# One load moved to another queue, a third of one product moved ahead of two transposes, and copied norm columns, in a fused attention and MLP kernel

## The chip, the cores and the metric

The kernel runs on one core of a Trainium2 chip. Its time is the device time of one execution in microseconds (us); the span is the part of it that the profile covers, about 1.4 us less. PE is TensorE, DVE is VectorE, ACT is ScalarE, POOL is GpSimd, SP is SyncE, which here only issues DMAs. All times inside a run are counted from the start of the span.

## The reference, cut to what matters

```python
xn = layernorm(x)                                  # x: 2048 tokens x 448
q, k, v = split(xn @ wqkv)                         # 16 heads of 28
pq, pk = phi(q), phi(k)                            # phi(t) = where(t > 0, t + 1, exp(t)) + 1e-6
s = (pq @ (pk.T @ v)) / (pq @ sum(pk)) @ wo        # per head, linear attention
g = silu(relu(xn @ w1 + b1) ** 2 @ w2 + b2)        # 448 -> 1792 -> 448
out = x + s * g
```

The change touches only the first 12 us: 16 tiles of 128 tokens are loaded, normalised and transposed, and the first products (K = xn times the k part of wqkv, H = xn times w1) start on the first tiles.

## The kernel before

The program is a list of operations; a small scheduler written in the kernel fixes the order on each engine, and semaphores carry the dependences. DVE and PE run their lists in order, so an operation that waits holds up all behind it. The loads at the start:

```python
load_x(0, 1)                                     # tile 0, 112 KB, on SP
load_x(1, 2, "act").prio = -118                  # tile 1 on ACT's queue
twins = load_k("sp", w_qkv, A_wqkv, "wk", 384, 2 * D, later=True)   # wk: rows 0 to 383
load_x(2, 4)
dma("act", b1r[...], B_b1 ...)
load_w1("w1a", 0, 512, 2, [twins])               # two halves, then last 64 rows of wk, of w1a
load_x(4, 8)
load_w1("w1b", 512, 1024)
```

448 columns are three chunks of 128 and one of 64. The last 64 columns are kept twice (columns 384 to 447 and 448 to 511), so that two half-height matmuls can run side by side (the traces show such pairs issued 3 to 4 ns apart). This "twin" is made in one instruction from x:

```python
def ln_last(si):                                 # writes both copies: 64 columns of x, read twice
    add("dve", tensor_scalar(out=xn[:, si, 384:512], in0=x_tok[...64 columns, twice], subtract mean, times rstd))
def ln_twin(lo, hi, eng="dve"):                  # tiles 4 to 15: a copy of the 64 normalised columns
    add(eng, tensor_copy(xn[:, lo:hi, 448:512], xn[:, lo:hi, 384:448]))
```

The head of PE's list, and the order that DVE is held to ("st" statistics, "mv" their mean and variance, "xn" norm, "xd" twin, "xT3" the eviction of tile 3's transposes):

```python
warm(8, wide=True)                               # dummy matmuls
turn(0, 0, "act"); turn(0, 1, "act")             # tile 0: 2 + 2 transposes, ACT evicts them
turn(1, 0, "act")                                # T10: first two chunks of tile 1
mains(k0, (0,), ...); mains(k0, (1,), ...); mains(k0, (2,), ...)    # K of tile 0, three chunks
turn(1, 1, "act")
mains(k1, (0, 1), ...) ...
h_mains(2); head["xT2"] = pe_transpose(2, None, "act")
h_mains(3); head["xT3"] = pe_transpose(3, None, "dve")
rests(k0, k1) ...                                # the last 64 rows of K and H
pe_four(*second)                                 # H for tiles 2 and 3; needs xT2, xT3
("dve", "st0 mv0 st1 mv1 xn00 xn01 xd0 xn10 xn11 xd1 st2 mv2 st3 mv3 xd2 xn2 xd3 xn3 xT3")
```

After xT3 the scheduler's DVE order is: st4, the min of phi(K0), st5, the min of phi(K1), the max-add of phi(K0), that of phi(K1). The max-add (a SCALAR_TENSOR_TENSOR) is the last reader of K0's PSUM bank (the memory, `pb` in the profiles, that holds the results of a phase's products until they are read). PE wants that bank for the phase of H4 and H6, just after that of K2 and K3 (Kn is K of tile n, Hn the n-th 128 of H's 1792 columns, both counted from 0).

## Time and profile before

| | before |
|---|---|
| three runs | 141.20, 141.24, 141.33 us |
| PE busy | 136.6 us of 139.7 (98%) |
| chain that ended last | PE 95% |
| tile 0 / wk / tiles 2-3 / tiles 4-7 landed | 2.20 / 4.07 / 4.73 / 8.76 us |

The landings are the last of a load's semaphore increments in the trace. Next come two lines of the page: the busy part, and the chain of waits followed back from the last instruction, as shares by engine.

```profile
PE 136.6 (98%) x1255; PEld 68.0 (49%) x1255; DVE 92.2 (66%) x226; ACT 77.8 (56%) x152; POOL 25.0 (18%) x33
...
PE 95%; DVE 2%; DMA 2%; issue 0%; DVEq 0%
```

PE is the limit, so what counts is the time at which PE stands idle or starts late. The timeline of PE at the start (start, length, engine, line, operation, operands, count, idle before it):

```profile
3.27 0.63 PE L1062 MATMUL pb<-ones 128*128 128x512 bf16 x1
4.09 1.00 PE L528 MATMUL pb<-ident,xn 128*128 128x128 bf16 x6 [0.19 <-DVE xn L486]
4.92 0.81 PE L641 MATMUL pb<-w_qkv,xT 128*128 128x512 bf16 x3
5.57 0.28 PE L528 MATMUL pb<-ident,xn 128*128 128x128 bf16 x2
5.68 0.59 PE L641 MATMUL pb<-w_qkv,xT 128*128 128x512 bf16 x2
```

The last dummy matmul, six transposes (four of tile 0 and T10), K of tile 0, two more transposes, K of tile 1. Lengths include the pipeline: a group of three 512-column matmuls "lasts" 0.81 us, but the next group starts 0.65 us after it.

DVE a little later, and PE beside it:

```profile
8.36 0.42 DVE L537 COPY xT<-pb 128x512 bf16<-128x512 bf16 x1 [0.49 <-PE pb L528]
8.78 0.63 DVE L463 BATCH_NORM_STATS2 st<-x_tok 128x6 f32<-128x448 bf16 x1
...
10.25 1.28 DVE L629 SCALAR_TENSOR_TENSOR qk<-pb,qk 128x512 bf16<-128x512 f32 x2
```

```profile
8.48 2.06 PE L688 MATMUL pb<-xT,w 64*128 64x256 bf16 x32
10.38 1.03 PE L641 MATMUL pb<-w_qkv,xT 64*128 64x512 bf16 x8
11.24 1.03 PE L688 MATMUL pb<-xT,w 64*128 64x512 bf16 x8
```

The statistics of tile 4 start at 8.78, when DVE has done the eviction before them; their load landed just before (8.76). The first max-add, from 10.25, frees K0's bank at 10.95.

### The profile page before, as it was taken

To read this page: it belongs to the slowest core of one execution; us is meant where nothing else is said; L and a number is where in the kernel's file an instruction comes from. 1 tells how busy PE (TensorE), PEld (TensorE's weight loads), DVE (VectorE), ACT (ScalarE), POOL (GpSimd) and SP (SyncE) were. 2 spreads that over 40 slices of the span, in tenths; PEclk is the share of its full clock that TensorE was granted. 3 is DMA by queue.
4 is the path that set the end of the run, shared out by engine and by line. 5 is a ranking of instruction groups with operands and counts; after the bars stand their busy time and mean duration, and the time that the engine had idled before them with its cause. 6 is when DMAs were issued, how large, how long until landed. Compare 5 with 4: busy or idle time off the path is not lost.

```text
span 139.7 us, 3106 instructions
## 1 busy us (share of the span) xinstructions
PE 136.6 (98%) x1255; PEld 68.0 (49%) x1255; DVE 92.2 (66%) x226; ACT 77.8 (56%) x152; POOL 25.0 (18%) x33
## 2 busy tenths in 40 slices
PE   9999999999999999999999999999999999999992
PEld 2474444444444444444455455645555555555481
DVE  3989899799878994889995900329636071542653
ACT  4769787879988878979788912422033030301220
POOL 6000000000000000000893000000002328091770
DMA  6997367999723200000000148960000103111122
GB/s 190 247 335 219 77 170 186 356 276 144 131 52 70 60 6 0 0 19 5 0 0 0 42 120 169 175 107 0 0 0 5 66 0 101 35 66 66 38 99 68
DMA packets 20354, 12.91 MB, mean 92 GB/s; under 512 B 9524, under 2 KB 19956, under 8 KB 20340
## 3 DMA queue, kind: packets, MB, share of 16 engines
q1 hardware_dynamic: 18332, 11.52, 33.3%
q10 hardware_dynamic: 2008, 1.20, 4.3%
q8 instruction: 10, 0.16, 0.5%
q14 instruction: 4, 0.03, 0.1%
HBM read 8.78 MB, written 2.10 MB: 78 GB/s over the span
## 4 chain that ended last, share of the span: by engine, by line
PE 95%; DVE 2%; DMA 2%; issue 0%; DVEq 0%
PE pb L955 31%; PE pb L688 30%; PE pb L641 9%; PE pb L1021 8%; PE pb L722 7%; PE pb L672 6%; DMA x_tok<-in_A_x_dram 2%; PE pb L528 1%; PE pb L728 1%; DVE st L463 1%; PE pb L815 1%; PE pb L776 1%; PE pb L853 0%; DVE xn L991 0%; DVE mv L464 0%; PE pb L846 0%
## 5 line engine op out<-in xcount | busy, mean ns | idle before, releaser
L688 PE MATMUL pb<-xT,w 64*128 64x512 bf16 (+2 forms) x408 | 51.6, 365 | 0.0
L955 PE MATMUL pb<-w,r 64*128 64x448 bf16 (+3 forms) x406 | 44.9, 343 | 0.0
L697 ACT ACTIVATE r<-pb,b1f 128x512 bf16<-128x512 f32 x56 | 35.1, 688 | 4.2 <-PE pb L688 4.2
L688 PEld LDWEIGHTS pb<-xT,w 64*128 64x128 bf16 (+1 forms) x408 | 22.8, 94 | 22.5 <-ACT r L697 0.5
L955 PEld LDWEIGHTS pb<-w,r 64*128 64x128 bf16 (+1 forms) x406 | 22.8, 95 | 19.9 <-issue 0.7
L966 DVE TENSOR_TENSOR gbuf<-pb,b2b 128x448 bf16<-128x448 f32 (+1 forms) x16 | 9.2, 608 | 30.0 <-PE pb L955 30.0
L931 ACT ACTIVATE gbuf<-gbuf 128x448 bf16<-128x448 bf16 (+1 forms) x16 | 8.7, 565 | 36.0 <-DVE gbuf L966 35.5
L1000 POOL TENSOR_TENSOR xn<-xn,x_tok 128x448 bf16<-128x448 bf16 x15 | 15.0, 1032 | 46.3 <-DVE xn L991 46.3
L641 PE MATMUL pb<-w_qkv,xT 64*128 64x512 bf16 (+1 forms) x106 | 17.8, 376 | 0.0
L672 PE MATMUL pb<-xT,w_qkv 64*128 64x512 bf16 x84 | 15.5, 376 | 0.0
L705 DVE TENSOR_TENSOR r<-r 128x512 bf16<-128x512 bf16 x42 | 14.4, 418 | 0.0
L390 POOL MEMSET kvm<- 128x2048 bf16 x1 | 1.8, 1804 | 63.4 <-DVE zb L666 63.4
L1021 PE MATMUL pb<-msb,pqT 64*128 64x448 bf16 (+3 forms) x93 | 10.9, 343 | 0.0
L629 DVE SCALAR_TENSOR_TENSOR qk<-pb,qk 128x512 bf16<-128x512 f32 x16 | 10.6, 685 | 0.2
L463 DVE BATCH_NORM_STATS2 st<-x_tok 128x6 f32<-128x448 bf16 x16 | 9.3, 610 | 2.0 <-DMA x_tok<-in_A_x_dram 2.0
L991 DVE TENSOR_TENSOR xn<-pb,gbuf 128x448 bf16<-128x448 f32 (+2 forms) x17 | 9.2, 591 | 2.0 <-ACT gbuf L931 1.5
L619 ACT ACTIVATE qk<-pb 128x512 bf16<-128x512 f32 x16 | 8.9, 593 | 3.0 <-PE pb L641 2.5
L641 PEld LDWEIGHTS pb<-w_qkv,xT 64*128 64x128 bf16 (+1 forms) x106 | 6.7, 94 | 6.0 <-ACT xT L538 0.2
L722 PE MATMUL pb<-qk,xn 128*128 128x448 bf16 x48 | 9.3, 353 | 0.0
L619 ACT ACTIVATE pqT<-pb 128x512 bf16<-128x512 f32 x12 | 6.8, 597 | 3.2 <-PE pb L688 1.6
L672 PEld LDWEIGHTS pb<-xT,w_qkv 64*128 64x128 bf16 x84 | 6.0, 94 | 5.0
L706 ACT ACTIVATE r<-r 128x512 bf16<-128x512 bf16 x14 | 8.4, 637 | 0.0
(71 smaller groups left out, 99.7 us busy)
## 6 DMA issues: line engine op xcount, KB each, us to landing
out_dram<-xn SPq DMA_DIRECT2D x15, 112.0 KB, 1.7
w<-in_B_w_dram SPq DMA_DIRECT2D x1, 1568.0 KB, 10.0
x_tok<-in_A_x_dram SPq DMA_DIRECT2D x3, 448.0 KB, 3.8
xT<-rows ACTq DMA_DIRECT2D x6, 112.0 KB
w<-in_B_w_dram SPq DMA_DIRECT2D x1, 576.0 KB, 4.6
xT<-rows SPq DMA_DIRECT2D x5, 112.0 KB
w_o<-in_A_wo_dram SPq DMA_DIRECT2D x1, 392.0 KB, 11.3
w_qkv<-in_A_wqkv_dram SPq DMA_DIRECT2D x1, 384.0 KB, 3.6
```

Source lines behind the costliest of these rows:

```text
L463: add("dve", lambda e, _: e.bn_stats(st6[:, si, :], x_tok[:, si, :]), [("x", si)], [("st", si)], 0.58),
L619: add("act", lambda e, _: e.activation(out=slot, in_=src(), func=AF.Exp), [buf, "actw"], [tile], 0.6)
L629: lambda e, _: e.scalar_tensor_tensor(out=slot, in0=src(), scalar=1.0 + 1e-6, in1=slot, op0=ALU.add, op1=ALU.max),
L641: return e.matmul(ps(b)[:, 0:512], xT[half[h], c, si * P : (si + 1) * P], w_qkv[half[h], c, 384 : 2 * D], start=start, stop=stop,)
L672: return e.matmul(ps(b)[:, 0:512], w_qkv[half[h], c, m * P : (m + 1) * P], xT[half[h], c, g * 512 : (g + 1) * 512], start=start, stop=stop,)
L688: return e.matmul(ps(b)[:, c0 : c0 + n], w_1[half[h], c, fi * P : (fi + 1) * P], xT[half[h], c, t : t + n], start=start, stop=stop,)
L697: lambda e, _: e.activation(out=slot, in_=ps(b)[:, 0:512], func=AF.Relu, bias=b1f[:, fi : fi + 1]),
L705: return e.tensor_tensor(out=slot, in0=slot, in1=slot, op=ALU.mult)
L722: last = e.matmul(ps(b)[:, 0:D], xn[:, si, c * P : (c + 1) * P], pk_of(si), start=(si == 0), stop=(si == NT - 1),)
L955: return e.matmul(ps(b)[:, 0:n], r2[half[h], fi, si * P : (si + 1) * P], w_2[half[h], fi, c], start=start, stop=stop)
L1000: eng, lambda e, _: e.tensor_tensor(out=ob, in0=ob, in1=x_tok[:, si, c], op=ALU.add),
L1021: return e.matmul(ps(b)[:, 0:n], q, m, start=start, stop=stop)
```

## The change

The intent: tile 0 should not share the DMA engines with tile 1 and land sooner; since tile 1 then comes later, a third of K0 fills the time ahead of its transposes; and copies of normalised columns should be cheaper than a second norm.

```diff
-        load_x(1, 2, "act").prio = -118
+        load_x(1, 2)
...
-            c = (slice(0, D if si > 3 else 384), slice(0, 256), slice(256, 384))[...]
+            c = (slice(0, D), slice(0, 256), slice(256, D if si else 384))[...]
...
-            twin = head[f"xd{i}"] = ln_last(i)
+            twin = head[f"xd{i}"] = ln_twin(i, i + 1, "dve") if i else ln_last(i)
...
         warm(8, wide=True)
+        warm(2)
...
+        mains(k0, (0,), [("xT", 0, "a")] + wnames("wk")[:1])
         turn(1, 0, "act")
-        mains(k0, (0,), [("xT", 0, "a")] + wnames("wk")[:1])
...
-            ("dve", "... st3 mv3 xd2 xn2 xd3 xn3 xT3"),
+            ("dve", "... st3 mv3 xn2 xd2 xn3 xd3 xT3"),
```

More of the change, by code (lines that the diff above doesn't have):

```diff
@@ L482, in ln_norm @@
         def ln_norm(si, part=None):
-            c = (slice(0, D if si > 3 else 384), slice(0, 256), slice(256, 384))[0 if part is None else part + 1]
+            c = (slice(0, D), slice(0, 256), slice(256, D if si else 384))[0 if part is None else part + 1]
             return add(
@@ L1108, in bass_recurrent_scan__linear_attn_block__dense_activation_squared_relu__prompt_kernel @@
         for eng, names in (
-            ("dve", "st0 mv0 st1 mv1 xn00 xn01 xd0 xn10 xn11 xd1 st2 mv2 st3 mv3 xd2 xn2 xd3 xn3 xT3"),
+            ("dve", "st0 mv0 st1 mv1 xn00 xn01 xd0 xn10 xn11 xd1 st2 mv2 st3 mv3 xn2 xd2 xn3 xd3 xT3"),
             ("act", "ln0 ex0 ln1 ex1 xT00a xT00 xT01 xT10 xT11 ln2 ex2 ln3 ex3 b1 xT2"),
```

## The prediction

> **What bounds it.** TensorE. The page gives PE 98% busy, the chain of waits 95% PE. From 8.8 us to the end I find no PE gap over 0.1 us in the matmul records, so only the first 8.8 us can move; a shift there should pass to the end one for one. That head (timeline, chain of waits) is: x tile 0 lands at 2.20; its statistics, Ln, Exp and normalise run to 4.04 (DVE/ACT); six transposes 4.09 to 4.92, each waiting for DVE; then PE is back to back (216 ns per 512-column matmul) from T10 at 4.80 to 8.16. Two fixed gaps follow: 0.10 us at 8.16, and 0.14 at 8.70, where PE waits for tile 3's eviction on DVE (8.36 to 8.78).
>
> **The queue move.** x tile 1 was issued on ACT at 0.16 us, its packets start at 1.53, while tile 0's run from 1.01 to 1.89. The Trainium skill (Trainium Kernel Development and Optimization, Key Constraints) says queues of different engines share the same 16 DMA engines and interleave; this trace agrees: both queues' packets are mixed from 1.53 to 1.85. Behind tile 0 on SP they cannot mix: estimate, three packets of 41 ns per engine, so tile 0 lands 0.12 us earlier (2.08), and tile 1 at 2.4 to 2.7, no later than the start of its statistics (2.98 before, about 2.86 then). Cost: one more issue of about 0.45 us on SP delays all later SP issues. wk 4.07 to about 4.4, x tiles 2-3 4.73 to 5.1, first w1 part 5.40 to 5.8, x tiles 4-7 8.76 to about 9.2. The first three should still be in time. Statistics of tile 4 already wait for their load (DVE at 8.78), so DVE there slips by 0.4; the K0 phi (ends 10.95) then releases its PSUM bank at 11.35, where PE wants it at 11.43. That slack is nearly eaten: 0 to 0.1 us.
>
> **The PE order.** K0's first third needs the xT eviction that ended at 4.79, so moving ahead of T10 gains only 0.07 us (4.92 to 4.85), while T10 moves from 4.80 to 5.07 and its eviction from 5.14-5.52 to 5.39-5.77. K1 then starts at 5.83 in place of 5.68: PE loses 0.14 us, to be set against tile 0's 0.12. Two narrow warm matmuls fill idle time, worth nothing.
>
> **The norm columns.** Tiles 1-3 replace a 0.31 us tensor_scalar by a 64-column copy (estimate 0.15 from the 0.20 of the 128-column copy), but it waits for the norm before it. For tiles 2, 3 the norm now comes first, so transposes may start 0.2 us earlier; yet PE reached those transposes late (slack 0.22 and 0.24), so it gains nothing.
>
> **Sum.** -0.12 + 0.14 + 0.03 = about +0.05; as DMA start-up may gain more than I count, I put it at 141.2 us, 140.9 to 141.55. Faster by over 2%: 0.01; within 2%: 0.98; slower: 0.01.
>
> **What would show it.** Tile 0 landing near 2.1; first transpose near 3.97; T10 after K0's first matmul; a 0.1 us gap before K1's first matmul; xn of tile 2 ahead of its twin and no PE wait there; statistics of tile 4 waiting to 9.2; a possible PE wait near 11.4.
>
> **What would make it wrong.** Tile 1 landing after 2.9, which delays tile 0's norm too, since DVE runs tile 1's statistics first. The TensorE clock: in the records matmuls run at half rate (427 ns per 512 columns) until about 4.8 us; K0's first third may fall in that stretch (+0.1 to 0.2). wk or x 2-3 landing later than 4.8 and 5.2.

## More of the kernel before

The waits of PE's weight loads (PEld) between 8 and 13 us are only this:

```profile
PEld pb L688 <- DVE xT L537: 0.3, 1, 0.3
```

## The result, and the profile after

Six runs of the changed kernel: median 141.66 us (141.41 to 141.71). Six of the kernel before: median 141.30 (141.20 to 141.58). The ratio is 1.0018, with a 95% interval of 1.0005 to 1.0031. A ratio here is the mean time of one kernel's fast runs over the mean of the other's in the same rounds, so it is not quite the ratio of the medians. The class "within 2%" was right; the time lay outside the stated range.

The same two lines of the page, of the changed kernel:

```profile
PE 136.9 (98%) x1257; PEld 68.5 (49%) x1257; DVE 92.1 (66%) x226; ACT 78.1 (56%) x152; POOL 25.0 (18%) x33
...
PE 97%; ACT 1%; DVE 0%; issue 0%; DVEq 0%
```

PE's timeline at the start:

```profile
3.27 0.85 PE L1062 MATMUL pb<-ones 128*128 128x512 bf16 x3
4.03 0.68 PE L528 MATMUL pb<-ident,xn 128*128 128x128 bf16 x4
4.74 0.39 PE L641 MATMUL pb<-w_qkv,xT 128*128 128x512 bf16 x1
4.96 0.28 PE L528 MATMUL pb<-ident,xn 128*128 128x128 bf16 x2
5.08 0.59 PE L641 MATMUL pb<-w_qkv,xT 128*128 128x512 bf16 x2
5.51 0.28 PE L528 MATMUL pb<-ident,xn 128*128 128x128 bf16 x2
5.72 0.60 PE L641 MATMUL pb<-w_qkv,xT 128*128 128x512 bf16 x2
```

Tile 0 landed at 2.15 instead of 2.20, so the transposes start 0.06 us sooner. K0's first third now stands before T10 (4.74). In the matmul records the last of the two transposes at 5.51 is issued at 5.564 and would be through in 0.053 us; K1 starts at 5.716, which is the 0.10 us gap foretold. K1 is 0.03 us later than before. DVE and PE further on:

```profile
8.39 0.42 DVE L537 COPY xT<-pb 128x512 bf16<-128x512 bf16 x1 [0.56 <-PE pb L528]
9.34 0.63 DVE L463 BATCH_NORM_STATS2 st<-x_tok 128x6 f32<-128x448 bf16 x1 [0.53 <-DMA x_tok<-in_A_x_dram]
...
10.80 1.28 DVE L629 SCALAR_TENSOR_TENSOR qk<-pb,qk 128x512 bf16<-128x512 f32 x2
```

```profile
8.51 2.06 PE L688 MATMUL pb<-xT,w 64*128 64x256 bf16 x32
10.41 1.03 PE L641 MATMUL pb<-w_qkv,xT 64*128 64x512 bf16 x8
11.54 1.04 PE L688 MATMUL pb<-xT,w 64*128 64x512 bf16 x8
```

Tiles 4-7 landed at 9.32. DVE stood idle 0.53 us for them, with phi(K0) behind it in line, and freed the bank at 11.50. PE's phase moved from 11.24 to 11.54. The waits of the weight loads, 8 to 13 us, have a new line:

```profile
PEld pb L688 <- DVE qk L629: 0.6, 1, 0.6
PEld pb L688 <- DVE xT L537: 0.3, 1, 0.3
```

0.6 us is the weight load's idle time. In the matmul records the lost time is 0.27 us: K2/K3's last matmul at 11.059 should be followed at 11.272, and is at 11.545. With the 0.03 of the head this is 0.30 of the 0.34 us by which the spans differ (139.65 and 139.99); from the bank phase to the last matmul the traces take 125.55 and 125.56 us. The page's chain of the changed kernel names an ACT instruction (L697) at this place instead of DVE; that instruction ended at 11.552, after the phase had started, so it cannot have released it. This pair of traces would close the case, but it was one pair, and it turned out to be an untypical one.

### The profile page after: what moved, and what is told of

It reads as the page before. It is cut to its first block, busy times and chain, and to the rows that moved or that the text cites. A ratio compares the mean times of both kernels' runs of the same rounds, so it can differ in the third digit from the quotient of the medians.

```text
span 140.0 us, 3110 instructions
## 1 busy us (share of the span) xinstructions
PE 136.9 (98%) x1257; PEld 68.5 (49%) x1257; DVE 92.1 (66%) x226; ACT 78.1 (56%) x152; POOL 25.0 (18%) x33
## 3 DMA queue, kind: packets, MB, share of 16 engines
HBM read 8.78 MB, written 2.10 MB: 78 GB/s over the span
## 4 chain that ended last, share of the span: by engine, by line
PE 97%; ACT 1%; DVE 0%; issue 0%; DVEq 0%
PE pb L955 30%; PE pb L688 30%; PE pb L641 8%; PE pb L1021 8%; PE pb L722 7%; PE pb L672 6%; PE pb L1062 3%; PE pb L728 1%; ACT r L697 1%; PE pb L528 1%; PE pb L815 1%; PE pb L776 1%; PE pb L853 0%; DVE xn L991 0%; PE pb L846 0%
## 5 line engine op out<-in xcount | busy, mean ns | idle before, releaser
L697 ACT ACTIVATE r<-pb,b1f 128x512 bf16<-128x512 f32 x56 | 35.2, 688 | 4.1 <-PE pb L688 4.1
```

What stands on the lines that cost most here:

```text
L697: lambda e, _: e.activation(out=slot, in_=ps(b)[:, 0:512], func=AF.Relu, bias=b1f[:, fi : fi + 1]),
```

## The experiments

All runs gave correct results. The eighteen runs are fourteen edited kernels, one of them twice, the kernel before once more and the changed one twice more. All ratios are to runs of before on the same chip. Runs counted as slow, over 1.5% above the fastest of the same kernel (two of e8, one each of e9 and e11) are left out of them.

### Parts of the change, one by one

`e1_queue` is before with `load_x(1, 2)`, nothing else:

```diff
-        load_x(1, 2, "act").prio = -118
+        load_x(1, 2)
```

> The kernel before with only the queue move (x tile 1 behind tile 0 on SP). Theory A (the loss is x tiles 4-7 landing about 0.55 us later, their statistics standing ahead of the K0 phi on DVE, and so PE waiting for K0's PSUM bank): x 4-7 land at 9.2 to 9.4, PE waits 0.25 to 0.4 us for the bank and goes on at about 11.5, as in the changed kernel; the time is that of the changed kernel, +0.2 to +0.4 us over before. Rival B (the loss is K0's first third ahead of T10, with K1 waiting for the eviction of T10): this kernel is no slower than before, 0 to 0.06 us faster.

Measured: 1.0032 (1.0019 to 1.0045), median 141.72. The time came out about as theory A had it (a little over its range), but not by the way it named. Tile 0 landed at 2.11; tiles 4-7 at 9.20; yet PE did not wait for the bank, because it had lost more earlier. Wk landed at 4.67 and tiles 2-3 at 5.31. Two of the waits of the weight loads, 4 to 9 us (the first counts also the wait for the first tile):

```profile
PEld pb L528 <- DVE xn L486: 1.6, 4, 1.0
PEld pb L688 <- DMA w<-in_B_w_dram: 0.2, 1, 0.2
```

Tile 3's transposes waited 0.15 us for the norm that followed the late tiles 2-3, and the clock was still at half rate in K0's first matmul.

`e2_order` is before with the PE order and `warm(2)`:

```diff
+        warm(2)
+        mains(k0, (0,), ...)
         turn(1, 0, "act")
-        mains(k0, (0,), ...)
```

> The kernel before with only the PE order (K0's first third ahead of T10) and the two narrow warm matmuls. Theory A: x 4-7 land at 8.75 as before, no PE wait near 11.4; but a gap of about 0.10 us before K1's first matmul, and T10 0.07 us of idle earlier, so +0.08 to +0.15 us over before. Rival B: +0.25 to +0.4 us.

Measured: 1.0014 (1.0002 to 1.0026). No wait near 11.3, the K1 gap is there (0.10 us). From the first transpose to the start of the second half of the first H products it took 4.79 us, against 4.76 before: only 0.03 us by the trace, less than the +0.08 expected.

`e3_cols` is before with the norm columns of the change (the three lines of the diff that name `slice`, `ln_twin` and the DVE order).

> The kernel before with only the norm columns changed (copies for tiles 1 to 3). Both theories: no PE wait is touched, 0.0 us within 0.06. Rival C (the longer DVE chain of copies costs the time): +0.2 us or more, with a PE wait at the transposes of tiles 2 or 3.

Measured: 1.0018 (1.0005 to 1.0032). By the trace nothing was lost: the same stretch took 4.74 us. The time does not fit that stretch, which is why the null test below was made.

### Taking the x 4-7 wait away

`e4_x4early` is the changed kernel with

```diff
-        load_w1("w1a", 0, 512, 2, [twins])
-        load_x(4, 8)
+        load_w1("w1a", 0, 512, 2, [twins, lambda: load_x(4, 8)])
```

> The changed kernel with the load of x tiles 4-7 issued ahead of the last 64 rows of the first w1 part, two SP issues earlier. Theory A: x 4-7 are issued at about 4.15 and land at 8.0 to 8.3, DVE does not wait for them, K0's bank is free by 10.98, the PE gap near 11.3 is gone, and the time is that of before +0.00 to +0.06 us (the head's +0.03 stays). Rival B: as slow as the changed kernel. Rival D (not the place in the issue queue but the DMA engines' load makes x 4-7 late): they still land after 9.0 and the gap stays.

Measured: 1.0025 (1.0013 to 1.0037). Half of the expectation held: tiles 4-7 landed at 8.57, and the gap near 11.3 was gone. But the last 64 rows of w1 now stood behind 448 KB on the same queue, landed at 8.78 and 9.03, and PE waited for them (a gap of 0.35 us ending at 9.08). The wait moved; it did not vanish, so the time settles nothing. Rival D is out, since the landing moved with the place on the queue; rival B, which also expected an unchanged time, is not.

`e7_phifirst` is the changed kernel with DVE's list reordered after scheduling:

```diff
+        d[at0 : at0 + 6] = [ts0, stt0, st4, ts1, st5, stt1]     # phi(K0), then tile 4's statistics, then the rest
```

> The changed kernel with DVE's statistics of tile 4 put behind the K0 phi, all else in place. Theory A: x 4-7 still land at 9.1 to 9.4, but DVE ends the K0 phi at 10.3 to 10.6 instead of 11.5, the PE gap near 11.3 is gone, no new gap appears, and the time falls by 0.2 to 0.3 us against the changed kernel, to before -0.1 to +0.1 us. Rival D (DMA or head alone): as slow as the changed kernel.

Measured: 1.0005 (0.9984 to 1.0026). Tiles 4-7 landed at 9.17, phi(K0) ended at 10.68, and there is no wait near 11.3. The whole waits of the weight loads, 8 to 15 us, are again one line:

```profile
PEld pb L688 <- DVE xT L537: 0.3, 1, 0.3
```

This trace cannot tell how much was won, since PE came 0.33 us late by its own head: wk landed at 4.83, and K0 waited for it although tile 0 had come at 2.03. The timeline names the load:

```profile
4.97 0.46 PE L641 MATMUL pb<-w_qkv,xT 128*128 128x512 bf16 x1 [0.32 <-DMA w_qkv<-in_A_wqkv_dram]
```

### The null test, and the changed kernel again

`e5_before_again` is the kernel before, `e6_after_again` and `e12_after_third` the changed one, with no edit.

> The kernel before, unchanged, as a null test and for a second trace of it. The first five traces show x tile 0 landing at 2.20, 2.36 and 2.39 us where tile 1 is on ACT and at 2.15, 2.11, 2.13 where it is behind tile 0. All theories: ratio 1.000 within 0.0013; tile 0 lands at 2.20 to 2.40; PE has no gap over 0.05 us between 9 and 74 us. If the ratio is off by more than 0.0013, the differences of about 0.2 us seen so far are not to be read from times at all, only from traces.

> The changed kernel again, for a second trace. Theory A: tile 0 lands at 2.08 to 2.18; x 4-7 land at 9.1 to 9.4; K1's first matmul is preceded by a gap of about 0.10 us; PE waits near 11.3 for K0's bank, by 0.27 us less whatever PE lost before that point (a later PE waits less, since DVE's end is set by the landing); the wait ends at 11.3 to 11.6. Time +0.15 to +0.4 us over before.

> The changed kernel a third time, beside the candidates on one chip. Theory A: tile 0 lands at 2.0 to 2.2, wk at 4.2 to 4.9, x 2-3 at 4.9 to 5.5, x 4-7 at 9.1 to 9.4; PE goes on at the landing of x 4-7 plus 2.23 us near 11.4, unless it arrives later than that by its own head. Over before by 0 to 0.4 us.

The null test gave 1.0015 (0.9992 to 1.0037), just outside the bound set for it, with runs from 141.15 to 142.22. So differences of 0.2% between two kernels cannot be read from these times alone. e6 gave 1.0000 (0.9982 to 1.0018), e12 1.0009 (0.9993 to 1.0025). The trace of e5 shows one source of the scatter. Its K0 group:

```profile
5.16 1.36 PE L641 MATMUL pb<-w_qkv,xT 128*128 128x512 bf16 x3
```

Against 0.81 us before: its matmuls are issued every 427 ns instead of 216. The clock of TensorE was still at half rate until 6.2 us in this execution, and until about 4.7 in the first trace of the same kernel. The Trainium skill (TensorE: Matmul & The Clock Gate, Part 1: The HAM clock gate) says that the array starts at half rate and that a free-running window of 3.4 us decides when it is released, so that the moment differs from run to run. The traces agree.

In e6 PE waited 0.12 us for the bank (11.437, the landing at 9.211 plus 2.226), in e12 not at all, since it came later by a cold start.

### A dose larger than the noise

`e9_x4late` is before, every other engine's order kept, with the load of tiles 4-7 behind w1b on SP:

```diff
+        d[at0 : at0 + 4] = [w1b main, w1b last rows, w1b last rows, x4]     # SP's list, after scheduling (in words)
```

> A dose, larger than the noise: the kernel before with the load of x tiles 4-7 three SP issues later (behind the second w1 part), every engine's order unchanged. Theory A: in the two traces of the changed kernel PE resumed 2.226 us after that load landed (9.319 and 11.545; 9.211 and 11.437). So here the load lands at 10.0 to 10.9, PE resumes 2.2 to 2.3 us after it, after a gap of 0.8 to 1.7 us near 11.3 (less what PE lost earlier), and the time is 0.7 to 1.6 us over before. If the statistics did not stand before the K0 phi in a way that matters, the time is that of before.

Measured: 1.0151 (1.0126 to 1.0176), median 143.58. The load landed at 11.99, later than expected, and PE went on at 14.217, 2.228 us after it. Here the chain of waits shows the whole mechanism (start, length, what):

```profile
6.77 5.22 DMA x_tok<-in_A_x_dram
...
12.01 0.63 DVE st L463
12.64 0.19 DVE qk L622
12.83 0.53 DVE st L463
13.37 0.19 DVE qk L622
13.56 0.61 DVE qk L629
...
14.22 0.39 PE pb L688
```

Load, statistics of tile 4, min of K0, statistics of tile 5, min of K1, max-add of K0, PE. The delay is the same 2.226 to 2.228 us in all three traces in which PE waited for the bank. This trace also has a late clock (half rate to 9.4 us), so its gap was 0.50 us; without that it would have been about 2.97 (14.217 less 11.245), which is an estimate.

### Trying to keep the early tile 0 without its costs

`e8_pooltwins` moves the four loads of last rows to GpSimd (`eng2="pool"`, and `"pool" if parts > 1 else "sp"` in `load_w1`), with the queue move, the norm columns, and tile 3's transposes one matmul earlier.

> A candidate: the queue move and the norm columns, T10 ahead of K0 as before, the four loads of the last 64 rows of wk and w1 issued by GpSimd once its masks are made, and tile 3's transposes one matmul earlier. Theory A: tile 0 lands near 2.13; SP issues x 4-7 near 2.9, so they land before 8; the last 64 rows land by 8.2; no PE gap near 11.3; the gap before the second half of the first w1 products falls from 0.14 to below 0.05; 0.1 to 0.35 us faster than before. If GpSimd's issue is slow, a PE gap near 8.3 eats it. If x 4-7 crowd the first w1 part or wk, gaps near 5 or 6.2.

Measured: 1.0279 (1.0257 to 1.0302), slower. GpSimd issued the four loads from 3.21 to 5.44 us, but they landed at 8.62, 10.08, 11.11 and 11.55, that is 5.4 to 6.7 us after their issue. SP's own loads were no faster there: tiles 4-7, issued at 2.92, landed at 9.01, and three loads issued between 3.44 and 4.53 landed 6.8 to 7.2 us later. So the late landings cannot be put down to GpSimd's issue alone. PE waited 1.64 and 1.25 us for the last rows. Across these waits the clock fell: the matmuls ran at half rate again from 11.6 to 14.3 (the trace's clock record has 0.5 from 10.98 to 14.39).

`e10_gate` leaves tile 1 on ACT and makes its issue wait for GpSimd's first constant; `e11_gate_t3` adds the norm columns and the earlier transposes of tile 3:

```diff
-        load_x(1, 2, "act").prio = -118
+        x1 = load_x(1, 2, "act"); x1.prio = -118
+        x1.deps.add(<the memset of eps5 on POOL>)
```

> The kernel before with x tile 1 still on ACT, but its issue held back by about 0.3 us (it waits for GpSimd's first constant), so that its packets start when tile 0's are nearly done, and SP has no extra issue. Theory A: tile 0 lands at 2.0 to 2.2 as behind the queue move, wk, x 2-3 and x 4-7 land as before (near 4.0, 4.8, 8.8), tile 1 at 2.6 to 2.8; no PE gap near 11.3; 0.05 to 0.25 us faster than before by the head, within the noise of the rounds.

> The candidate: the held-back issue, the norm columns of the change, and tile 3's transposes one matmul earlier. On top of the run with the held-back issue alone, the gap before the second half of the first w1 products falls from 0.14 to 0.05 us or less. 0.1 to 0.4 us faster than before. If x 2-3 land after 5.2, tile 3's transposes wait and the gain is gone.

Both expectations were wrong: 1.0103 (1.0066 to 1.0141) and 1.0059 (1.0013 to 1.0105). Tile 0 did land at 2.13, but tile 1 at 3.73 and 3.53. The held issue (0.43 instead of 0.16 in e10) did not hold back its packets: they started at 1.50, against 1.53 before. But they went on beside those of wk until about 3.2, where before they were through by about 2.2; why they were slower is open. Since DVE has tile 1's statistics ahead of tile 0's norm, the first transposes came late, and PE stood idle before them:

```profile
4.88 1.11 PE L530 MATMUL pb<-ident,xn 128*128 128x128 bf16 x6 [0.98 <-DVE xn L488]
5.78 1.06 PE L643 MATMUL pb<-w_qkv,xT 128*128 128x512 bf16 x2
```

The clock then came at about 9.4 us. The runs fall in two groups, for example 141.18 and 141.53 against four of 142.95 to 143.80 in e11. The group at 143 was not profiled run by run, so that the clock divides the two groups is likely, not shown.

`e13_nomove` is the changed kernel with only the queue move undone; `e14_warm2` is before with `warm(2)` alone.

> The changed kernel with the queue move alone undone (tile 1 on ACT again). Theory A: tile 0 lands at 2.2 to 2.4, wk at 3.7 to 4.1, x 2-3 at 4.6 to 5.1, x 4-7 at 8.75 to 8.9; no PE wait near 11.3; K1 still preceded by a 0.10 us gap; 0.0 to +0.15 us over before, at or under the changed kernel. If the order or the columns carry the cost, it is as slow as the changed kernel or slower.

> The kernel before with the two narrow warm matmuls alone. In the run that held tile 1 back, PE stood 1.2 us idle before its first transpose and the clock reached full rate only at 9.4 us; in the six traces with the two narrow ones it came between 3.1 and 5.6, in the five of the queues of before or the moved queue without them and no other delay, between 3.9 and 6.2. If the idle stretch matters, no run of this kernel is over 141.9 and its mean is 0 to 0.15 us below before; if it doesn't, the same as before, 0.0 within 0.1 us.

e13: 1.0023 (1.0009 to 1.0037), slower than expected and no better than the changed kernel. Tile 0 landed at 2.25, wk at 4.12, tiles 4-7 at 8.64, no wait near 11.3, the K1 gap of 0.10. So the queue move may not be the only part that costs. The two runs that have the PE order without the move were 0.14% and 0.23% over before, but the first is within what the null test showed for no change at all, the second has the norm columns too, and the traces show 0.03 us (e2) to 0.2 us (e13, where K0's first matmul at 4.90 was still at half rate). A cost of the order beyond that is not shown. e14: 1.0000 (0.9987 to 1.0014), with all five runs between 141.25 and 141.44. The warm matmuls changed nothing in the mean that these runs can show; whether they narrow the scatter stays open.

### A version that was faster in its runs

The norm columns alone gain nothing, but they end tile 3's norm earlier. PE can use that: `e15_t3warm` is before with the norm columns, `warm(2)`, and

```diff
-        h_mains(3)
-        head["xT3"] = pe_transpose(3, None, "dve")
+        h_mains(3, (0, 1))
+        head["xT3"] = pe_transpose(3, None, "dve")
+        h_mains(3, (2,))
```

`e16_best2` adds the queue move and the DVE order of e7. `e17_t3warm_again` repeats e15, and `e18_t3only` is e15 with the norm columns of before.

> Candidate: the queues and PE order of before, the norm columns of the change, the two warm matmuls, and tile 3's transposes one matmul earlier. The gap of 0.14 us before the second half of the first w1 products falls to 0.05 or less, nothing else changes: 0.05 to 0.25 us faster than before.

> Candidate: as the last, with the queue move and with tile 4's statistics behind the K0 phi on DVE. Tile 0 lands 0.2 us earlier than on the queues of before, no wait near 11.3; but wk at 4.3 to 4.8 and x 2-3 at 4.9 to 5.5 may hold K0 or tile 3's transposes. If they do not bite, 0.2 to 0.4 us faster than before; if they do, 0 to 0.2.

> The candidate of the earlier run again. If its gain is real: 0.1 to 0.35 us faster than before, the gap before the second half of the first w1 products at 0.03 again. If it was scatter: 0.0 within 0.1.

> The same with the norm columns of before: tile 3's norm ended 0.26 us later there (7.88 against 7.62 in the first traces), and its transposes would now be wanted at about 7.83 with a first tile landing at 2.20, so PE waits up to 0.1 us for the norm ahead of them, and gains 0.0 to 0.08 us over before in place of 0.11. If the columns don't matter, no such wait and the gain of the candidate.

e15: 0.9985 (0.9972 to 0.9997). e17: 0.9971 (0.9950 to 0.9992), six runs within 141.04 to 141.18. The gap before the second half of the first H products fell from 0.14 to 0.03 us in both. Over both sets, 11 runs average 141.13 us; 65 runs of the kernel before, in all sets, average 141.48 (141.47 for the 20 beside them). That is 0.34 us, with an uncertainty of 0.13, and more than the 0.11 us of the gap. The rest goes with a smaller scatter of these runs (141.03 to 141.30) and is not explained.

e18: 0.9992 (0.9968 to 1.0016). PE at tile 3's transposes, first e17, then e18 (the second line of each is those transposes):

```profile
7.68 0.38 PE L688 MATMUL pb<-xT,w 128*128 128x256 bf16 x2
7.90 0.39 PE L528 MATMUL pb<-ident,xn 128*128 128x128 bf16 x4
```

```profile
7.80 0.38 PE L688 MATMUL pb<-xT,w 128*128 128x256 bf16 x2
8.12 0.40 PE L528 MATMUL pb<-ident,xn 128*128 128x128 bf16 x4
```

Two matmuls of 0.109 us are the first line. In e17 the transposes follow at once (7.68 to 7.90); in e18 they come 0.10 us late (7.80 to 8.12), for the norm, as expected. So the new order of the columns is worth something, once PE's list asks for it: 0.10 us by the trace, 0.29 by the times of the same rounds, with an uncertainty of 0.12.

e16: 0.9995 (0.9983 to 1.0008). Tile 0 at 2.07, but behind it a new wait, where the bank no longer was one:

```profile
10.27 1.03 PE L641 MATMUL pb<-w_qkv,xT 64*128 64x512 bf16 x8
11.49 0.82 PE L688 MATMUL pb<-xT,w 64*128 64x512 bf16 x6 [0.20 <-ACT r L697]
```

The bracket names ACT, which had long been done; the sequencer's semaphore records show a wait to 11.33 on the last part of w1b, which landed at 11.29 (10.51 in the first trace of before). The same phase needs w1b. In the changed kernel w1b landed at 11.23, so removing the bank wait there would have left an estimated 0.16 us of the 0.27 (11.23 plus the 0.20 seen here, less 11.27).

### The traces side by side

Read from the traces, us: landings of tile 0, wk, tiles 2-3, tiles 4-7; first transpose (T); start of the second half of the first H products (H'); the phase that takes K0's bank (bank); start of the last half-rate matmul, dummies included (half).

```
run               x0    wk    x2-3  x4-7   T      H'      bank    half
before            2.20  4.07  4.73  8.76   4.086  8.842   11.245  4.53
e5 (before)       2.38  3.77  4.60  8.88   4.260  9.632   12.034  6.02
e3 columns        2.39  3.97  4.82  8.84   4.273  9.014   11.416  3.27
e14 warm2         2.38  3.96  5.01  8.68   4.257  9.011   11.413  3.80
e2 order          2.36  4.06  5.10  8.83   4.244  9.032   11.433  3.27
e13 order+columns 2.25  4.12  5.13  8.64   4.135  9.134   11.536  4.90
after             2.15  4.27  4.92  9.32   4.030  8.870   11.545  4.11
e6 (after)        2.12  4.51  5.30  9.21   4.001  8.916   11.437  none after 2.8
e12 (after)       2.12  4.28  4.93  9.09   4.003  9.265   11.667  5.38
e1 queue          2.11  4.67  5.31  9.20   3.992  9.080   11.482  4.89
e7 phi first      2.03  4.83  5.50  9.17   3.912  9.168   11.569  4.97
e17 best          2.30  3.98  4.80  8.95   4.181  8.808   11.210  3.80
e9 x4 late        2.48  3.96  5.29  11.99  4.366  11.310  14.217  9.43
```

In all rows but e7 (its DVE list is another) "bank" is, within 0.003 us, the later of two: H' plus 2.403, and the landing of tiles 4-7 plus 2.227. A late start by the head hides the wait for the bank, and the other way round. That is why costs of single parts do not add up here.

What comes after the bank phase has nothing to do with the change: to the last matmul all twenty traces take 125.55 to 125.56 us (e12 125.65). But the last store then takes 1.77 to 2.31 us from its issue to the end of the span, with no pattern by kernel. That alone can move a time by 0.5 us. It also accounts for the trace of e3: its span is 0.34 us over that of the first trace of before, 0.17 because its bank phase came that much later, after a first tile at 2.39, and 0.17 because of its last store.

## Why the prediction was right or wrong

- "The queue move ... tile 0 lands 0.12 us earlier": right in direction. The first pair shows 0.05. The rows above with tile 1 on ACT average 2.34 (2.20 to 2.48), those with it behind tile 0 2.11 (2.03 to 2.15). So the gain is about 0.24 us, and the first trace of before had the luckiest landing.
- "All later SP issues delayed by about 0.45": right. Issue of tiles 4-7 went from 4.96 to 5.43.
- "The first three should still be in time": wrong in three traces out of five with the move in the table. Wk (predicted 4.4) came at 4.27 to 4.83 and held K0 in e7; tiles 2-3 (predicted 5.1) came at 4.92 to 5.50 and held tile 3 in e1 and e6. This gave back what tile 0 had won.
- "That slack is nearly eaten: 0 to 0.1 us": this is the term of the sum that was mis-sized. It measured 0.27 us in the profiled pair. One part is the landing, 9.32 for 9.2. The larger part is that I took 11.43, close to the modelled end of the preceding phase (11.41), for the time at which PE wants the bank. PE issues the next phase 0.16 us before that end (11.245), and the traces show another 0.05 us from the release of the bank to the issue. So the slack was 0.26 us (11.245 less 10.98, the landing plus 2.227), not 0.48; the load came 0.56 us later and the head 0.03, which leaves the 0.27. In the two other traces of the changed kernel the wait was 0.12 (e6) and 0 (e12), as the head had lost more.
- "PE loses 0.14 us, to be set against tile 0's 0.12": the gap before K1 came as predicted, 0.10 us, in the change, e2 and e13. But both terms were smaller in the pair: from the first transpose to K1 it took 0.09 us longer (0.04 in e2), and the first transpose came 0.06 sooner. That they left +0.03, where the sum had +0.02, is luck.
- "Two narrow warm matmuls ... worth nothing": not contradicted; e14 is 1.0000 within 0.14%.
- "The norm columns ... gains nothing": right for the columns alone (4.74 us in e3 against 4.76); with the PE list adapted they carried part of a real gain (e17 against e18).
- "As DMA start-up may gain more than I count, I put it at 141.2": this shading had no measurement behind it and went the wrong way. The sum itself, +0.05, on the first median is 141.29.
- The range rested on three runs of before that lay within 0.13 us. In 65 runs that kernel takes 141.12 to 142.22 us, mean 141.48, and the traces show three sources of that: the landing of the first tile, the clock's release and the last store. Pooled over the rounds, 18 runs of the changed kernel average 141.58 and the 45 of before up to then 141.48: a difference of 0.10 us, with an uncertainty of 0.11. The first set's 0.18% is thus likely the upper side of a smaller effect, and the sign itself is not certain from times alone. (Weighting the three ratios by their intervals gives 0.11% with 0.09%, no firmer beside a null test of 0.15%.) The traces show its makeup: an earlier tile 0, spent on a gap before K1 and on loads that come later.

What stays open: how much of the 0.1 to 0.3% in e2 and e13 is the PE order itself and how much the moment at which the clock was released; and whether e3's 0.18% over six runs is more than the late first tile and last store of its trace.

## What to carry to other kernels

When a load is moved to a busier queue, list every later load on that queue with the moment it is needed and the operations that stand in line behind its first reader, since an in-order engine passes a late load on to work that never reads it. Measure slack to the issue of the next instruction, not to the modelled end of the one before it. Before predicting a change of 0.2%, find out what the same kernel's own runs scatter by, and look at more than one trace of it.

## What the Trainium skill lacked or had wrong

- TensorE: Matmul & The Clock Gate, Part 1: it gives the release at about 4 us into sustained matmul activity, give or take 0.5, and a penalty under 1% of a typical span. Here the dummy matmuls start at 0.30 us, and half rate lasted to anywhere from under 3.3 to 6.2 us of the span in executions without added idle, and to 9.4 us in three where the first transposes came late (4.37 to 4.88). In e10, one of the three, the stretch from the first transpose to the second half of the first H products took 6.60 us against 4.76 before, an estimated 1.3% of the 141.57 us of before.
- No page: the profile's view prints a granted clock of 1.00 in the first microseconds, where matmul issues of 427 ns for 512 columns show half rate. The traces hold no clock record there: the first one begins at the release (4.18 us in the changed kernel, 9.62 in e9), and five traces, that of before among them, have none. Without a record the issue distance has to be read.
- Trainium Kernel Development and Optimization, Key Constraints: it says that queues of SP, ACT and GpSimd share the 16 DMA engines and interleave. The traces agree; the size is missing there. 112 KB on ACT beside 112 KB on SP delayed the latter by about 0.24 us, and the same 112 KB, issued 0.3 us later beside the 384 KB of wk, landed about 1 us later (3.73 and 3.53, against 2.56 to 2.97 in the runs with tile 1 on ACT).
- DMA: Bandwidth & Descriptors, Specifications: it gives first bytes at about 1 us for loads issued by GpSimd and 0.6 for SP and ACT. What it lacks is the size of a backlog: beside a busy SP queue the first packet of GpSimd's loads started at 6.87 us, 3.7 us after the first issue, and loads of 32 and 64 KB landed 5.4 to 6.7 us after theirs (e8). SP's own loads of that stretch took 6.8 to 7.2, so the busy engines account for much of it; what held GpSimd's first packet, with nothing before it on its own queue, is open. In before the same loads from SP took 3.6 to 3.9 (medians of the page).
- TensorEngine Tiling (Array Packing) says that changing the tiling mode drains the array; the cost is not given. Here a step from 128-row to 64-row matmuls had a gap of about 0.10 us in every trace but e8, where PE waited there for a load.
